# Moving the kv sums next to other small matmuls, and z into 128x64 tiles, in a fused sketched-attention and GELU kernel

## The chip, the cores and the metric

The kernel runs on one core of a Trainium2 chip. The metric is the device time of one execution, in microseconds (us). Engines are called by the names of the profile: PE is TensorE, DVE is VectorE, ACT is ScalarE, POOL is GpSimd, SP is SyncE. PE multiplies matrices into PSUM, and a second row of the profile, PEld, shows its weight loads.

A float32 matmul of the kernel appears in the profile as two records. "128*64" in a row gives the tile of PE's array that a matmul uses: 128 rows (the length of the sum) by 64 columns (rows of the output). Two matmuls in 128*64 tiles, four in 128*32 tiles or eight in 64*32 tiles lie side by side in the array.

## The reference

Attention with polynomial sketches, and then a dense layer with GELU:

```python
def phi(x):                                   # x: (4, 4, 1088, 32), r = 8
    a = np.einsum('rd,bhsd->bhsr', S1, x)
    b = np.einsum('rd,bhsd->bhsr', S2, x)
    return np.einsum('bhsi,bhsj->bhsij', a, b).reshape(*x.shape[:-1], r * r)
q_p, k_p = phi(q), phi(k)
kv = np.einsum('bhsf,bhsd->bhfd', k_p, v)     # 64 x 32 for each batch and head
z = np.sum(k_p, axis=2)                       # 64 for each batch and head
num = np.einsum('bhsf,bhfd->bhsd', q_p, kv)
den = np.einsum('bhsf,bhf->bhs', q_p, z)[..., None] + 1e-06
x = num / den                                 # then (4352, 128)
h = x @ w_in                                  # (4352, 2048)
out = (0.5 * h * (1 + erf(h / sqrt(2)))) @ w_out
```

There are 4 batches (B) and 4 heads (H) of width 32 (D); F = 64 is the number of features, and a batch has 1088 tokens.

## The kernel before

**Chunks and steps.** Tokens are taken in nine chunks n. Chunks 0 to 7 have 512 tokens, two of them for each batch; chunk 8 holds the 64 remaining tokens of all batches. For each chunk the hidden layer is made in 16 slices fi of 128 channels. A step t is one slice of one chunk: `hidden` (line 686) multiplies a slice of w_in by the chunk's transposed activations xT into a PSUM bank h_ps (line 692, from step 18 on in two 128*64 halves), and ACT applies GELU to it (line 699). Chunks 0 and 1 share the first 32 steps; chunk n from 2 on has the steps 16n to 16n + 15. There are two h_ps banks, so the hidden of step t needs the gelu of step t - 2.

**The second layer.** From four gelu slices (a block) POOL makes four sums (`token_sums`, lines 741 to 744), and PE multiplies blocks and sums by parts of w_out in pairs of 128*64 matmuls (`two_products`, line 776). These products come some steps later, at the end of a step. DVE adds them up and stores the chunk.

**Attention.** For batches 1 to 3, `features_of_all` (line 945, 64*32 tiles) sketches a batch's keys, and DVE makes their features k_p (`outer_of_all`, lines 953 to 960) and their sum over the tokens of one partition, k_s (`add_tokens`, lines 969 to 975). PE then forms, head by head,

- kv: `kv_sum` (line 431), 32 + 4 matmuls in 128*32 tiles, 72 records, all through `kv_product` (line 428);
- z, spread over a head's 32 rows: `z_sum` (line 440), a matmul of 128*32 for each head, with ones as its stationary part and k_s as its moving part.

ACT copies kv out of PSUM (`take_kv`, line 453), PE turns it with an identity (`turn_kv`, line 458, 128*64) and ACT copies the result to kz (line 459). DVE multiplies z into the sketch weights (`fold_z`, which calls `sketch_of_z`, lines 483 to 486), and the result, S_abc, is the stationary part of `query_sketch` (line 568, 64*32 tiles). So a chunk's sketch also gives its denominators. `query_outer` (from line 580 on, DVE) makes the features of the queries, already divided; `attend` (line 617, 64*32 tiles) multiplies them by kz, and ACT copies the numerators to xT (line 623). Batch 0 has another way at the start; its z is turned by `turn_first_kv` (line 504) for use in chunk 8.

**Order.** Every engine keeps the order of the program text. A table of slots, filled by `at(t, ...)`, says what is issued in step t besides hidden and the products: in a step come the hidden matmul, then the slots in the order in which they were entered, then the products. Batch 1 has its entries in steps 12 to 28: `features_of_all`, `outer_of_all` in 16, `add_tokens` in 17, kv in 21, `turn_kv` in 22, z and `fold_z` in 23, `query_sketch` of chunk 2 in 24. For batches 2 and 3 the entries are relative to t = 32 and 64: kv and z at t + 13 in one function, `turn_kv` and `fold_z` at t + 14. An even chunk n has `attend` of chunk n - 1 and `query_sketch` of chunk n in the step before its first one; an odd one has `sketch_and_attend` there.

**PSUM.** There are eight banks: two h_ps, two o_ps for the products, and two pairs w_ps for all else (`work_banks`; `work_bank` gives the first of a pair). A third user of w_ps waits until one of the pairs is done with.

Of the kernel before, what the change touches and what calls it, by code (L numbers as in the profile page):

```python
# [8 lines left out]
FP = mybir.dt.float32  # L9
# [7 lines left out]
def kernel(  # L17
# [18 lines left out]
    pe, dve, act, pool, sp = nc.tensor, nc.vector, nc.scalar, nc.gpsimd, nc.sync  # L36
    B, H, S, D = q.shape
    R = S1.shape[0]
    F = R * R
# [3 lines left out]
    NP = H // 2  # L43
# [4 lines left out]
    CW = JC * 128  # L48
    G = 128 // 32
    NCH = J // JC  # L50
# [9 lines left out]
    big = ctx.enter_context(tc.tile_pool(name="big", bufs=1))  # L60
# [6 lines left out]
    def work_banks():  # L67

        return wps.tile([128, 2, CW], FP, name="w_ps")

    def work_bank():
        return work_banks()[:, 0]
# [7 lines left out]
    def out_bank():  # L80
        return ops.tile([128, CW], FP, name="o_ps")
# [137 lines left out]
    ident = big.tile([128, 128], FP, name="ident")  # L219
# [9 lines left out]

    kz_first = big.tile([128, 128], FP, name="kz_first")  # L230

    ones = big.tile([128, D], FP, name="ones")

    v_rem_aug = [big.tile([128, H, D if b else 2 * D], FP, name=f"v_rem_aug{b}") for b in range(B)]
    pool.memset(v_rem_aug[0], 0.0)
    pool.memset(v_rem_aug[0][:REM], 1.0)
    dve.memset(ones, 1.0)

    v_aug = [att.tile([128, NP, J, 2 * D], FP, name="sums") for r in range(2)]
    for t in v_aug:  # L240
# [165 lines left out]
    k_s = {}  # L406

    def flat(features):
        return features.rearrange("p i j -> p (i j)")
# [16 lines left out]
    def kv_product(ps, lhsT, features, h, part, start=False, stop=False):  # L426

        pe.matmul(ps[h * D:(h + 1) * D, part * F:(part + 1) * F], lhsT=lhsT, rhs=features, start=start, stop=stop,  # L428
                  skip_group_check=True)

    def kv_sum(b, ps):


        for i in range(J):
            for h in range(H):
                kv_product(ps, main["v", b][:, h, i, :], k_p[b][h // 2][:, i, h % 2], h, 0, start=i == 0)
        for h in range(H):
            kv_product(ps, v_rem_aug[b][:, h, :], flat(k_p_rem[b % 2][:, h]), h, 0, stop=True)

    def z_sum(b):  # L440

        ps = held["kv"][:, 0]
        for h in range(H):
            kv_product(ps, ones, k_s[b][:, h], h, 1, start=True, stop=True)

    def fold_z(b):
        sketch_of_z(b, held["kv"][:, 0], F)

    kv_T = {}

    def take_kv(b, ps):
        kv_T[b] = att.tile([128, F], FP, name="kv_T")
        act.copy(out=kv_T[b], in_=ps[:, :F])

    def turn_kv(b, banks):

        for rows in (slice(0, 64), slice(64, 128)):
            pe.matmul(banks[rows, 1, :128], lhsT=kv_T[b], rhs=ident, start=True, stop=True)
        act.copy(out=kz[b], in_=banks[:, 1, :128])
# [20 lines left out]
    def sketch_of_z(b, ps, at):  # L480

        zs = att.tile([128, R, R], FP, name="z_s")
        dve.tensor_mul(out=zs, in0=ps[:, at:at + F].rearrange("p (i j) -> p i j", i=R), in1=sT[:, None, R:].broadcast_to([128, R, R]))
        c = ps[:, 2 * F:2 * F + R]
        dve.tensor_reduce(out=c, in_=zs, axis=mybir.AxisListType.X, op=AX.add)
        dve.tensor_mul(out=S_abc[b][:, :, :, 4:8], in0=c.rearrange("p (i f) -> p i f", i=2)[:, :, None].broadcast_to([128, 2, 2, 4]),
                       in1=own_r[:, None, :, None].broadcast_to([128, 2, 2, 4]))
# [11 lines left out]
    def turn_first_kv():  # L499

        ps, zs = work_bank(), held["zs"]
        for h in range(H):
            c, r = h // 2, h % 2
            pe.matmul(ps[h * D:(h + 1) * D, :F], lhsT=zs[:, r], rhs=ident[:, c * F:(c + 1) * F], start=True, stop=True)
        sketch_of_z(0, ps, 0)


# [44 lines left out]
    def batch_of(n, s, i):  # L552
        return n // NCH if n < NMAIN else i * 2 + s
# [51 lines left out]
    def attend(n, banks=None):  # L605


        W = width[n]
        m = 1 if n < NMAIN else B // 2
        banks = work_banks() if banks is None else banks  # L610
        f = qp[n].rearrange("f r x -> f (r x)")[:, :2 * W].rearrange("f (c i n r t) -> f c i n r t", c=NP, i=m, r=2, t=32)
        N = W // 2 // m
        for i in range(m):
            for s in range(2):
                rows, b = slice(s * 64, (s + 1) * 64), batch_of(n, s, i)
                for h in range(H):
                    pe.matmul(banks[h * D:(h + 1) * D, s, i * N:(i + 1) * N],  # L617
                              lhsT=(kz[b] if b else kz_first)[rows, h * D:(h + 1) * D],
                              rhs=f[rows, h // 2, i, :, h % 2], start=True, stop=True)
        xT[n] = att.tile([128, CW], FP, name="xT", bufs=3)  # L620
        to = xT[n][:, :W]
        to = to.rearrange("p (s x) -> p s x", s=2) if m == 1 else to.rearrange("p (s t i) -> p s i t", s=2, i=m)
        act.copy(out=to, in_=banks[:, :, :W // 2] if m == 1 else banks[:, :, :W // 2].rearrange("p s (i t) -> p s i t", i=m))
# [238 lines left out]
    r = Rounding(SR)  # L862
# [12 lines left out]
    banks = [out_bank(), out_bank()]  # L875
# [59 lines left out]
    def at(t, f, *a):  # L935
        slots[t].append(lambda: f(*a))
# [40 lines left out]
    held = {}  # L977
# [11 lines left out]
    def features_rem(pair):  # L989
        key_features_rem(pair, held["rem"])  # L990

    def finish_keys(b, z=True):
        held["kv"] = work_banks()
        kv_sum(b, held["kv"][:, 0])
        if z:
            z_sum(b)
        take_kv(b, held["kv"][:, 0])

    def round_at(t, w, product_by=dve):
        r = []  # L1000
# [18 lines left out]
    at(17, add_tokens, 1)  # L1019
    at(18, channel_sums, 4)  # L1020

    at(21, finish_keys, 1, False)
    at(22, lambda: turn_kv(1, held["kv"]))
    at(23, z_sum, 1)
    at(23, fold_z, 1)
    at(23, query_turn, 3)
    at(24, query_sketch, 2)
    at(24, query_outer, 2)
    for i, t in enumerate((25, 26, 28)):
        at(t, channel_sums, i)  # L1030
# [2 lines left out]
    for n in range(3, NCHUNK):  # L1033

        t = (n - 1) * NF
        b = (n + 1) // 2
        keys = n % 2 and b < B
        if n > 3:
            at(t - 6, query_turn, n)
        if keys:  # L1040
            at(t - 1, sketch_and_attend, n)
            at(t - 1, features_of_all, b)
        else:
            at(t - 1, attend, n - 1)
            at(t - 1, query_sketch, n)
        at(t - 1, query_outer, n)
        if keys:
            for r in range(2):
                at(t - 3 if n > 3 else t - 4, key_turn_blocks, b, r)

        if n == NMAIN:
            at(t + 15, attend, n)
        if keys:
            at(t + 5 + (n == NCH + 1), outer_of_all, b)
            at(t + 5 + (n == NCH + 1), add_tokens, b)
            at(t + 8, widen_v_rem, b)
            at(t + 13, finish_keys, b)
            if b == 2:
                at(t + 13, turn_first_kv)
            at(t + 14, lambda b=b: turn_kv(b, held["kv"]))  # L1060
            at(t + 14, fold_z, b)


    products = {t: [] for t in range(len(steps) + LAG)}
# [2 lines left out]
    for t, (n, fi) in enumerate(steps):  # L1067
# [13 lines left out]
        elif fi % NB == NB - 1:  # L1081
            b = fi // NB
# [11 lines left out]
    for t in range(len(steps) + LAG):  # L1094
        if t < 4:
# [9 lines left out]
            if t == 3:  # L1105
                banks = work_banks()
# [23 lines left out]
        if t < len(steps):  # L1130
            n, fi = steps[t]
            hidden(n, fi, by_halves=t >= 18 and (n < NMAIN or fi < 5))
        if t < len(steps) and steps[t][0] < NMAIN and steps[t][1] % NB == NB - 1:
            n, b = steps[t][0], steps[t][1] // NB
# [50 lines left out]
```

## Time and profile before

| | |
|---|---|
| time, median of 3 runs | 260.33 us (260.18 to 260.61) |
| time of the profiled execution | 260.86 us |
| its span, first to last instruction | 259.1 us |
| granted clock of PE, mean | 0.999 |
| PE busy | 254.6 us, 98% of the span |
| POOL busy | 163.5 us, 63% |
| DVE busy | 151.6 us, 59% |
| ACT busy | 114.9 us, 44% |
| L428, kv and its remainder: 192 + 24 records of 128*32, 64 columns | 3.3 + 0.9 us |
| L428, z: 24 records of 128*32, 64 columns | 0.9 us |
| L504, turn of the first z: 8 records of 128*32, 64 columns | 0.3 us |
| L568, sketches of queries: 96 records of 64*32, 256 columns | 3.9 us |
| L617, numerators: 96 records of 64*32, 256 columns | 3.9 us |

The span is what the instructions cover; the execution's time has some 1.8 us more around it. Matmuls overlap: the ends in the profile are modelled, and what a group of matmuls takes from PE is read from the starts. A timeline gives start and length in us, engine, line, operation, the tiles written and read, the shape, the number of instructions merged into the row, and in brackets idle time of the engine and what ended it.

### The profile page before, as it was taken

The numbers are of one execution on the slowest core, as the hardware profiler recorded it, in microseconds if no ns is written. First come the engines' busy times: TensorE is split into PE (matmuls) and PEld (weight loads), VectorE is DVE, ScalarE is ACT, GpSimd is POOL, SyncE is SP. The second block draws the span as 40 slices with busy tenths as digits, with TensorE's granted clock in tenths as the row PEclk, the third lists the DMA queues.
The fourth block names the chain that finished last, engine by engine and source line by source line (L and its number), as shares of the span: only waits on it lengthen the run. The fifth ranks groups of instructions, "written<-read, shape, count | busy, mean of one in ns | idle before, by whom it ended". The sixth has DMA issues, their size and how long they took to land.

```text
span 259.1 us, 5758 instructions
## 1 busy us (share of the span) xinstructions
PE 254.6 (98%) x2335; PEld 134.8 (52%) x2335; DVE 151.6 (59%) x313; ACT 114.9 (44%) x221; POOL 163.5 (63%) x173
## 2 busy tenths in 40 slices
PE   8999999999999999999999999999999999999994
PEld 7856444344444554444444454444445444445794
DVE  2886879969698997680178957630565043600330
ACT  4675767432625333533335334533353335334431
POOL 3404006799968776687758766867768776877200
PEclk9999999999999999999999999999999999999999
DMA  6469849820000101001000011020001100010020
GB/s 205 137 192 360 206 95 220 217 54 13 3 0 13 30 4 28 13 12 31 3 0 3 0 27 17 3 41 0 3 0 25 19 4 0 14 29 0 3 41 20
DMA packets 29530, 13.48 MB, mean 52 GB/s; under 512 B 21824, under 2 KB 27712, under 8 KB 29504
## 3 DMA queue, kind: packets, MB, share of 16 engines
q1 hardware_dynamic: 29472, 13.12, 20.8%
q8 instruction: 18, 0.29, 0.5%
q14 instruction: 8, 0.07, 0.1%
q10 hardware_dynamic: 32, 0.00, 0.0%
HBM read 10.88 MB, written 2.23 MB: 51 GB/s over the span
## 4 chain that ended last, share of the span: by engine, by line
PE 98%; ACT 0%; issue 0%; DVE 0%
PE h_ps L692 45%; PE o_ps L776 33%; PE o_ps L827 5%; PE w_ps L824 3%; PE w_ps L428 2%; PE w_ps L857 1%; PE w_ps L617 1%; PE w_ps L568 1%; PE o_ps L417 1%; PE w_ps L534 1%; PE h_ps L706 1%; PE h_ps L333 1%; PE w_ps L945 1%; PE w_ps L635 0%; PE w_ps L333 0%; PE h_ps L373 0%
## 5 line engine op out<-in xcount | busy, mean ns | idle before, releaser
L692 PE MATMUL h_ps<-xT,w_in 128*64 128x512 f32 (+3 forms) x514 | 137.1, 576 | 0.0
L699 ACT ACTIVATE block<-h_ps 128x512 f32<-128x512 f32 (+1 forms) x128 | 73.0, 571 | 120.2 <-PE h_ps L692 119.8
L776 PE MATMUL o_ps<-block,w_out 128*64 128x256 f32 x224 | 57.5, 379 | 0.0
L692 PEld LDWEIGHTS h_ps<-xT,w_in 128*64 128x64 f32 (+1 forms) x514 | 41.9, 142 | 29.2 <-issue 11.6
L741 POOL TENSOR_TENSOR bits_low<-block 128x512 f32<-128x512 f32 x28 | 35.6, 1273 | 27.6 <-ACT block L699 27.6
L776 PEld LDWEIGHTS o_ps<-block,w_out 128*64 128x64 f32 x224 | 30.5, 137 | 37.5 <-issue 26.7
L742 POOL TENSOR_TENSOR bits_a<-block 128x512 f32<-128x512 f32 x28 | 35.7, 1276 | 12.8 <-ACT block L699 12.8
L743 POOL TENSOR_TENSOR bits_e<-bits_a,block 128x512 f32<-128x512 f32 x28 | 36.1, 1290 | 2.2
L744 POOL TENSOR_TENSOR bits_m<-block,bits_e 128x512 f32<-128x512 f32 x28 | 35.8, 1280 | 2.2
L580 DVE STREAM_TRANSPOSE w_ps<-w_ps 128x512 f32<-128x512 f32 (+1 forms) x7 | 4.9, 693 | 42.8 <-PE w_ps L568 30.1
L776 PE MATMUL o_ps<-bits_low,small 128*64 128x256 f32 x112 | 29.0, 381 | 0.0
L776 PE MATMUL o_ps<-block,small 128*64 128x256 f32 x112 | 28.9, 381 | 0.0
L776 PE MATMUL o_ps<-bits_a,small 128*64 128x256 f32 x112 | 28.8, 379 | 0.0
L776 PE MATMUL o_ps<-bits_m,w_out 128*64 128x256 f32 x112 | 28.7, 379 | 0.0
L776 PEld LDWEIGHTS o_ps<-block,small 128*64 128x64 f32 x112 | 15.0, 137 | 17.6 <-issue 10.2
L791 DVE COPY sums<-o_ps 64x256 f32<-64x256 f32 x8 | 3.3, 416 | 34.4 <-PE o_ps L776 34.4
L776 PE MATMUL o_ps<-bits_e,small 128*64 128x256 f32 x112 | 17.1, 384 | 0.0
L827 PE MATMUL o_ps<-g,w_out 128*128 128x512 f32 (+1 forms) x34 | 16.5, 572 | 0.0
L776 PEld LDWEIGHTS o_ps<-bits_m,w_out 128*64 128x64 f32 x112 | 15.3, 137 | 0.0
L776 PEld LDWEIGHTS o_ps<-bits_a,small 128*64 128x64 f32 x112 | 15.2, 137 | 0.0
L776 PEld LDWEIGHTS o_ps<-bits_low,small 128*64 128x64 f32 x112 | 15.0, 137 | 0.0
L776 PEld LDWEIGHTS o_ps<-bits_e,small 128*64 128x64 f32 x112 | 7.5, 136 | 10.6 <-issue 9.1
(181 smaller groups left out, 303.2 us busy)
## 6 DMA issues: line engine op xcount, KB each, us to landing
out_dram<-oT SPq DMA_DIRECT2D x26, 64.0 KB, 2.2
block<-in_moe_w_in_dram SPq DMA_DIRECT2D x3, 512.0 KB, 7.2
block<-in_moe_w_out_dram SPq DMA_DIRECT2D x3, 512.0 KB, 11.6
k<-in_k_dram SPq DMA_DIRECT2D x12, 128.0 KB, 2.8
v<-in_v_dram SPq DMA_DIRECT2D x12, 128.0 KB, 3.4
q<-in_q_dram SPq DMA_DIRECT2D x24, 64.0 KB, 2.3
k<-in_k_dram SPq DMA_DIRECT2D x2, 256.0 KB, 2.8
q<-in_q_dram SPq DMA_DIRECT2D x2, 256.0 KB, 4.1
```

Source lines behind the costliest of these rows:

```text
L428: pe.matmul(ps[h * D:(h + 1) * D, part * F:(part + 1) * F], lhsT=lhsT, rhs=features, start=start, stop=stop, skip_group_check=True)
L580: dve.transpose(out=tok, in_=ps[:, :, :H2])
L692: pe.matmul(ps[rows, :W], lhsT=w[:, rows], rhs=xT[n][:, :W], start=True, stop=True)
L699: act.activation(out=g_of[n, fi][:, :W], in_=ps[:, :W], func=ACT.Gelu)
L741: pool.tensor_sub(out=s[3], in0=a11, in1=a21)
L742: pool.tensor_add(out=s[1], in0=a21, in1=a22)
L743: pool.tensor_sub(out=s[2], in0=s[1], in1=a11)
L744: pool.tensor_sub(out=s[4], in0=a12, in1=s[2])
L776: pe.matmul(acc[n][bank][half * 64:(half + 1) * 64, col:col + HW], lhsT=fixed, rhs=moving, start=opens and e == 0 and name in "4715", stop ...
L791: dve.tensor_copy(out=N[lo, 0, one], in_=a0[lo, one])
L824: pe.matmul(o_of[n][i][:, :128], lhsT=g[:, i * 128:(i + 1) * 128], rhs=w_tile(w_out_sb, fi), start=first, stop=final)
L827: pe.matmul(o_of[n][:, cols], lhsT=w_tile(w_out_sb, fi), rhs=g[:, cols], start=first, stop=final)
```

## The change

kv and z of a batch are no longer one function. kv is issued directly ahead of other matmuls in 32-column tiles, into a free part of their PSUM pair: in step 24 ahead of `query_sketch` of chunk 2 (batch 1), and in the steps 47 and 79 ahead of `attend` of chunks 3 and 5, which `query_sketch` of chunks 4 and 6 follows (batches 2 and 3). `turn_kv` comes two steps after it, instead of one.

z stays in step 23 for batch 1 and in steps 45 and 77 for the others, with a PSUM pair of its own. Its stationary part is now 64 columns wide: ones for one head of a pair and noughts for the other, and the two matmuls of a pair are added up in PSUM, so that there are still four matmuls. `fold_z` follows in the same step. The turn of the first z goes from four matmuls with 32 columns to two with 64, one step later.

```diff
--- before.py
+++ after.py
@@ -229,12 +229,13 @@
 
     kz_first = big.tile([128, 128], FP, name="kz_first")
 
-    ones = big.tile([128, D], FP, name="ones")
+    ones = big.tile([128, 3, D], FP, name="ones")
 
     v_rem_aug = [big.tile([128, H, D if b else 2 * D], FP, name=f"v_rem_aug{b}") for b in range(B)]
     pool.memset(v_rem_aug[0], 0.0)
     pool.memset(v_rem_aug[0][:REM], 1.0)
-    dve.memset(ones, 1.0)
+    dve.memset(ones, 0.0)
+    dve.memset(ones[:, 1], 1.0)
 
     v_aug = [att.tile([128, NP, J, 2 * D], FP, name="sums") for r in range(2)]
     for t in v_aug:
@@ -439,12 +440,14 @@
 
     def z_sum(b):
 
-        ps = held["kv"][:, 0]
-        for h in range(H):
-            kv_product(ps, ones, k_s[b][:, h], h, 1, start=True, stop=True)
+        held["z"] = work_bank()
+        for r in range(2):
+            for c in range(NP):
+                pe.matmul(held["z"][c * F:(c + 1) * F, :F], lhsT=ones[:, 1 - r:3 - r].rearrange("p a d -> p (a d)"),
+                          rhs=k_s[b][:, 2 * c + r], start=r == 0, stop=r == 1)
 
     def fold_z(b):
-        sketch_of_z(b, held["kv"][:, 0], F)
+        sketch_of_z(b, held["z"], 0)
 
     kv_T = {}
 
@@ -499,9 +502,9 @@
     def turn_first_kv():
 
         ps, zs = work_bank(), held["zs"]
-        for h in range(H):
-            c, r = h // 2, h % 2
-            pe.matmul(ps[h * D:(h + 1) * D, :F], lhsT=zs[:, r], rhs=ident[:, c * F:(c + 1) * F], start=True, stop=True)
+        for c in range(NP):
+            pe.matmul(ps[c * F:(c + 1) * F, :F], lhsT=zs.rearrange("f r d -> f (r d)"), rhs=ident[:, c * F:(c + 1) * F],
+                      start=True, stop=True)
         sketch_of_z(0, ps, 0)
 
 
@@ -989,12 +992,13 @@
     def features_rem(pair):
         key_features_rem(pair, held["rem"])
 
-    def finish_keys(b, z=True):
-        held["kv"] = work_banks()
-        kv_sum(b, held["kv"][:, 0])
-        if z:
-            z_sum(b)
-        take_kv(b, held["kv"][:, 0])
+    def kv_and_attend(b, n):
+
+        banks = held["kv"] = work_banks()
+        kv_sum(b, banks[:, 1, CW // 2:])
+        if n >= NCH:
+            attend(n, banks)
+        take_kv(b, banks[:, 1, CW // 2:])
 
     def round_at(t, w, product_by=dve):
         r = []
@@ -1019,12 +1023,12 @@
     at(17, add_tokens, 1)
     at(18, channel_sums, 4)
 
-    at(21, finish_keys, 1, False)
-    at(22, lambda: turn_kv(1, held["kv"]))
     at(23, z_sum, 1)
     at(23, fold_z, 1)
     at(23, query_turn, 3)
+    at(24, kv_and_attend, 1, 1)
     at(24, query_sketch, 2)
+    at(26, lambda: turn_kv(1, held["kv"]))
     at(24, query_outer, 2)
     for i, t in enumerate((25, 26, 28)):
         at(t, channel_sums, i)
@@ -1033,7 +1037,7 @@
     for n in range(3, NCHUNK):
 
         t = (n - 1) * NF
-        b = (n + 1) // 2
+        b = (n + 1) // 2 if n % 2 else n // 2
         keys = n % 2 and b < B
         if n > 3:
             at(t - 6, query_turn, n)
@@ -1041,7 +1045,11 @@
             at(t - 1, sketch_and_attend, n)
             at(t - 1, features_of_all, b)
         else:
-            at(t - 1, attend, n - 1)
+            if n % 2 == 0 and b < B:
+                at(t - 1, kv_and_attend, b, n - 1)
+                at(t + 1, lambda b=b: turn_kv(b, held["kv"]))
+            else:
+                at(t - 1, attend, n - 1)
             at(t - 1, query_sketch, n)
         at(t - 1, query_outer, n)
         if keys:
@@ -1054,11 +1062,10 @@
             at(t + 5 + (n == NCH + 1), outer_of_all, b)
             at(t + 5 + (n == NCH + 1), add_tokens, b)
             at(t + 8, widen_v_rem, b)
-            at(t + 13, finish_keys, b)
+            at(t + 13, z_sum, b)
+            at(t + 13, fold_z, b)
             if b == 2:
-                at(t + 13, turn_first_kv)
-            at(t + 14, lambda b=b: turn_kv(b, held["kv"]))
-            at(t + 14, fold_z, b)
+                at(t + 14, turn_first_kv)
 
 
     products = {t: [] for t in range(len(steps) + LAG)}
```

## The prediction

> **What bounds the kernel now.** I read the page first: TensorE carries the chain that ended last, so a change counts by what it adds to or takes from PE's own queue, or by letting PE stand still.
>
> ```profile
> PE 254.6 (98%) x2335; PEld 134.8 (52%) x2335; DVE 151.6 (59%) x313; ACT 114.9 (44%) x221; POOL 163.5 (63%) x173
> ...
> PE 98%; ACT 0%; issue 0%; DVE 0%
> ```
>
> Second, PE's timeline where batch 1 is finished (steps 21 to 25). Columns: start, length, then what ran; the time that a run of matmuls holds PE is the distance to the next start, since ends overlap.
>
> ```profile
> 50.28 1.06 PE L692 MATMUL h_ps<-xT,w_in 128*64 128x512 f32 x4
> 51.27 1.10 PE L428 MATMUL w_ps<-k_p,v 128*32 128x64 f32 x64
> 52.19 0.29 PE L428 MATMUL w_ps<-k_p_rem,v_rem_aug 128*32 128x64 f32 x8
> 52.41 1.08 PE L692 MATMUL h_ps<-xT,w_in 128*64 128x512 f32 x4
> 53.32 0.39 PE L458 MATMUL w_ps<-ident,kv_T 128*64 128x128 f32 x4
> 53.54 1.03 PE L692 MATMUL h_ps<-xT,w_in 128*64 128x512 f32 x4
> 54.50 0.32 PE L428 MATMUL w_ps<-k_s,ones 128*32 128x64 f32 x8
> 54.75 0.43 PE L776 MATMUL o_ps<-block,small 128*64 128x256 f32 x1
> ...
> 56.09 1.03 PE L692 MATMUL h_ps<-xT,w_in 128*64 128x512 f32 x4
> 57.05 0.66 PE L568 MATMUL w_ps<-qT,S_abc 64*32 64x256 f32 x16
> 57.65 0.43 PE L776 MATMUL o_ps<-block,w_out 128*64 128x256 f32 x1
> ```
>
> To be seen: no gap anywhere, and the price of a tile size. Four hidden records (L692) take 0.86 among 128*64 work (58.56 to 59.42); 0.96 ahead of another size (53.54 to 54.50); 0.91 just after one (52.41 to 53.32). The kv run is 18 groups of four records; 64 of them take 0.92, which is 0.056 a group and 0.02 at the start, so 1.01 of work, and the run holds PE 1.14.
>
> Third, VectorE's timeline in the same place, which decides this forecast.
>
> ```profile
> 49.07 4.07 DVE L969 TENSOR_REDUCE w_ps<-k_p 128x128 f32<-128x1024 f32 x2
> 53.18 0.43 DVE L974 COPY k_s<-w_ps 64x256 f32<-64x256 f32 x1
> 53.62 0.42 DVE L975 TENSOR_TENSOR k_s<-w_ps,k_p_rem 64x256 f32<-64x256 f32 x1
> 54.96 0.22 DVE L483 TENSOR_TENSOR z_s<-w_ps,sT 128x64 f32<-128x64 f32 x1 [0.92 <-PE w_ps L428]
> ```
>
> The token sums k_s of batch 1, which z multiplies, are ready at 53.62 + 0.42 = 54.04. VectorE has had no idle time since the transpose at 44.67, all of it fed by PE work before 47. z starts on PE at 54.50, some 0.4 after its operand.
>
> **What the Trainium skill says.** "TensorEngine Tiling (Array Packing)", Tiling Modes, Key Properties: changing the tiling mode drains TensorE. The trace agrees: 0.10 before, 0.13 to 0.16 at the other end, 0.05 in the first pair after it. "TensorE: Matmul & The Clock Gate", Part 1 (engine queue depths): PE may pull weight loads ahead, but matmuls stay in order. So nothing behind a waiting z can pass it; that a wait stops the queue isn't seen here, since PE hardly waits. Same page and part: the clock falls only after about 3.4 us without work. The granted clock is 9 tenths or more in all slices; the wait that I expect is a third of that.
>
> **The change, part by part.**
>
> *Price of a separate small run.* 128*32 (kv, z): 0.10 before + 0.02 in its first group + 0.11 at its end + 0.05 after = 0.29. 64*32 (sketches): L568 holds PE 0.60 for 0.43 of work (69.01 to 69.44 is a run in the middle of such work), so 0.10 + 0.16 + 0.05 = 0.31.
>
> *kv beside sketches or numerators (three times).* The 72 records stay. Two separate runs cost 0.29 + 0.31 = 0.60. Merged, there are three switches: into 128*32 (0.12), from 128*32 to 64*32 (unknown), out (0.14 + 0.05). The unknown is not in the trace. Below: 0, if only the rows are split and the columns stay 32. Above: 0.14, the 0.11 at the end of a kv run and 0.025 for the next start. Nearest row: from 64*64 to 32*64, also a change of rows alone:
>
> ```profile
> 12.11 0.67 PE L635 MATMUL h_ps<-kz,q_pT 64*64 64x33 f32 x32
> 12.60 0.65 PE L635 MATMUL o_ps<-kz,q_pT 64*64 64x33 f32 x32
> 13.17 0.69 PE L534 MATMUL w_ps<-qT,Srep 32*64 32x256 f32 x16
> ```
>
> The first 32 records take 0.49, with a switch at their start; the last 32 take 0.57 with one at their end. A change of rows alone is therefore not free (about 0.11). I take 0.14: each merge saves 0.60 − 0.45 = 0.15.
>
> *z in 128x64 tiles.* Still 8 records, now in two tiles instead of four: four pairs instead of two groups. L417 (128*64, 33 columns) runs 16 pairs from 10.16 to 11.16, 0.06 a pair, so z is 0.24. For batch 1 it loses a run of its own: 0.11 + 0.29 = 0.40 before, 0.24 after, −0.16. For batches 2 and 3, where z stood inside the kv run: +0.13 each. The turn of the first z goes from 8 records to 4: two pairs for two groups, 0.12 for 0.11, nothing.
>
> *The cover that z loses.* kv (1.14 + 0.10 + 0.05) leaves step 21 and turn_kv (53.32 to 53.54, 0.22) leaves step 22; both stood ahead of z(1) in PE's queue, which stays in step 23. Hidden of step 21 ends at 51.27 − 0.10 = 51.17; two more at 0.86 bring PE to z at 52.9, or 53.1 if step 23 must wait for the bank of step 21's gelu (it ends about 52.1). But k_s is there only at 54.04, since VectorE's work is the same. With 0.1 to wake, z starts at 54.15: **PE stands about 1.1 us**, and with it the products of step 23, the hidden of 24, kv and the sketches. ACT's next gelu waits for these; POOL's token sums (gapless from 49.34 to 59) have their inputs.
>
> *Batch 1 summed.* z from 54.15, 0.03 for an unloaded start, 0.24: products start at 54.42, not 54.75 (−0.33). They no longer follow a switch (−0.05). kv comes ahead of the sketches (+1.14, their 0.60 unchanged): the sketches end 0.76 later. turn_kv in step 26: +0.22. **+0.98**.
>
> *Batches 2 and 3.* k_s is ready at 93.05 and 148.47, z came at 95.29 and 151.5 and would come at 94.3 and 150.4: no wait. Each −0.15 + 0.13: **−0.02**, twice.
>
> *Costed at nothing.* The second memset of ones (0.09 like the first): VectorE then waits 2.54 for S; without that, 0.1. The copy kv_T on ACT (0.21) follows the copy xT that hidden needs, and turn_kv comes two steps later; if it came before, up to 0.2. query_outer(2) ends 0.76 later, at 65.0, and its features are used at about 70. fold_z: only a query transpose (0.71) is queued behind it. Banks: in batch 2 the first z's fold ended at 99.08 and kv needs a bank at 99.4; it should get that of z, free at 98.6. No DMA moves, SP and POOL get nothing new.
>
> Sum: 0.98 − 0.04 = +0.94. The profiled execution (260.86, span 259.1) becomes 261.8 with a span of 260.0; on the median 260.33, which is 0.53 below the profiled one, **261.25**.
>
> **The rivals.**
> A, as above: 261.25, own range 260.95 to 261.6.
> B, z waits but the rows-only switch is free: 3 × 0.14 less, +0.52, 260.85. Same columns speak for it, the rows above against.
> C, z(1) doesn't wait: then only the switches count, 0.98 becomes −0.31, in all −0.36: 259.97, not slower. Its place is k_s against the end of hidden in step 23. The point: the sum is nought when the wait is 0.2 instead of 1.1, that is with k_s by about 53.2. VectorE's unbroken chain speaks against it, as does z's slack of only 0.4.
> D, one more wait: kv or the sketches of batches 2 and 3 find their bank not yet freed by the folds, which VectorE ends 0.2 to 0.8 before (99.08 against 99.4): up to 0.5 in all, 261.7. Against: both engines shift together.
>
> **How the numbers follow.** A 0.66, B 0.12, C 0.10, D 0.12. About 0.2% (0.5 us) is what a measurement of this kernel tells from no change. Slower: A, D and a part of B, 0.80; same: the rest of B and most of C, 0.16; faster 0.04 (C with a free switch, 259.55). Range 260.7 to 261.7: A, most of B and half of D, with 0.1 to 0.2 either way for the median.
>
> **What would show it.** The timeline after: L692 of steps 18 to 23 with no L428 between; a gap of 1.0 to 1.2 before L428 with k_s, put down to VectorE's k_s (L975) and not to an issue; L428 of kv followed by L568 after about 1.14, or 1.01 if B is right; L504 with 4 records; batches 2 and 3 without gaps. I am wrong if k_s is ready earlier, if PE is busy until 54, or if the gap lies elsewhere.

## The result and the profile after

The changed kernel takes 262.4 us (median of 6 runs, 261.68 to 262.63), the kernel before on the same chip 260.56 (6 runs, 260.18 to 261.15). The ratio is 1.0067 with a 95% interval from 1.0050 to 1.0084: slower by about 1.75 us by that ratio, which is not simply the quotient of the two medians. The forecast was 261.25, with a range of 260.7 to 261.7. The direction was right, the forecast size was about half of the measured one, and the measured time lies above the range. The profiled execution took 262.53 us and has a span of 260.7.

The page of the changed kernel, busy times and the chain that ended last:

```profile
PE 254.8 (98%) x2331; PEld 135.4 (52%) x2331; DVE 151.6 (58%) x314; ACT 114.8 (44%) x221; POOL 163.3 (63%) x173
...
PE 92%; DVE 5%; issue 1%; ACT 1%; DVEq 0%
```

PE is as busy as before, in absolute terms. What changed is the chain: it was 98% PE, now 5% of it runs over VectorE. So PE has begun to wait for VectorE. Busy shares alone would not have shown it.

Lines have moved: in the kernel after z is L446, kv L429, hidden L695, the products L779, the sketches L571, the numerators L620, `turn_kv` L461, the second half of k_s L978 and the end of a fold L489.

PE's timeline where batch 1 is finished, kernel after (start, length, what ran, idle time before and what ended it):

```profile
50.42 2.94 PE L695 MATMUL h_ps<-xT,w_in 128*64 128x512 f32 x12
54.17 0.45 PE L446 MATMUL w_ps<-k_s,ones 128*64 128x64 f32 x8 [0.81 <-DVE k_s L978]
54.45 0.38 PE L779 MATMUL o_ps<-block,small 128*64 128x256 f32 x1
...
55.75 1.03 PE L695 MATMUL h_ps<-xT,w_in 128*64 128x512 f32 x4
56.71 1.10 PE L429 MATMUL w_ps<-k_p,v 128*32 128x64 f32 x64
...
57.85 0.45 PE L571 MATMUL w_ps<-qT,S_abc 64*32 64x256 f32 x8
```

The same from 53.2 on, where the first row holds the last two hidden matmuls alone, and VectorE's timeline beside it:

```profile
52.76 0.60 PE L695 MATMUL h_ps<-xT,w_in 128*64 128x512 f32 x2
```

```profile
53.70 0.42 DVE L978 TENSOR_TENSOR k_s<-w_ps,k_p_rem 64x256 f32<-64x256 f32 x1
```

This is the forecast wait: the hidden matmuls run through without kv between them. The last two of them start at 52.76 and take 0.43 (half of the 0.86 for four), so z could follow at 53.19. It starts at 54.17, 0.05 after the end of k_s (53.70 + 0.42). PE stands 0.98. The bracket says 0.81, since the lengths of matmuls are modelled and reach beyond the next possible start. kv follows further down, and from its start to that of the sketches it takes 57.85 − 56.71 = 1.14, what it took ahead of 128*64 work before. So the change from 128*32 to 64*32, rows alone, costs here what a change of columns cost.

The second wait is in batch 2. The kernel before first, PE's timeline and one row of VectorE's, the end of the fold of batch 2's z:

```profile
94.26 1.10 PE L428 MATMUL w_ps<-k_p,v 128*32 128x64 f32 x64
...
95.63 0.43 PE L776 MATMUL o_ps<-block,small 128*64 128x256 f32 x1
...
97.40 0.39 PE L458 MATMUL w_ps<-ident,kv_T 128*64 128x128 f32 x4
...
99.44 0.66 PE L617 MATMUL w_ps<-q_pT,kz 64*32 64x256 f32 x16
```

```profile
98.47 0.17 DVE L486 TENSOR_TENSOR S_abc<-w_ps,own_r 128x16 f32<-128x16 f32 x1
```

The same of the kernel after:

```profile
98.11 1.03 PE L695 MATMUL h_ps<-xT,w_in 128*64 128x512 f32 x4
99.75 1.10 PE L429 MATMUL w_ps<-k_p,v 128*32 128x64 f32 x64 [0.60 <-PE h_ps L695]
...
100.89 0.66 PE L620 MATMUL w_ps<-q_pT,kz 64*32 64x256 f32 x16
```

Its VectorE, and its row of PE's sequencer at line 429 between 94 and 101 (durations in ns: shortest, median, longest):

```profile
98.13 0.71 DVE L841 STREAM_TRANSPOSE oT<-sums 128x512 f32<-128x512 f32 x1
98.88 0.23 DVE L486 TENSOR_TENSOR z_s<-w_ps,sT 128x64 f32<-128x64 f32 x1
99.14 0.23 DVE L488 TENSOR_REDUCE w_ps<-z_s 128x8 f32<-128x64 f32 x1
99.47 0.17 DVE L489 TENSOR_TENSOR S_abc<-w_ps,own_r 128x16 f32<-128x16 f32 x1
99.56 0.21 DVE L486 TENSOR_TENSOR z_s<-w_ps,sT 128x64 f32<-128x64 f32 x1
```

```profile
L429 PEldq EVENT_SEMAPHORE  x3: 51/51/3177, 96.3 to 96.5; - x3
```

Four hidden records ahead of another tile size take 0.96, here 1.63 (98.11 to 99.75): PE stands 0.67. The sequencer held a semaphore for 3.18 us, from 96.5 to 99.69. Just before that, at 99.64 (99.47 + 0.17), VectorE ended the fold of batch 2's z (the first L489); the fold of the first z, which begins at 99.56, was still running when kv started. The bracket names PE's own hidden work as the releaser, which isn't it: hidden was done by 99.14 (98.11 + 1.03). The wait was for several semaphores, and by its time that of VectorE came last; an experiment below tests it. z had taken one pair of w_ps, the first z the other, and kv had to wait until VectorE had read z's. VectorE came to it late, since it stored chunk 1 first (up to L841).

Where the 1.64 us between the two spans are, from the starts of PE's work at the same points in both: 0.14 up to step 18 (the start, of which the experiments say more), 0.88 in batch 1, 0.65 in batch 2, −0.03 in batch 3. Between these points the two kernels keep step.

### The profile page after: what moved, and what is told of

Same layout as the page of the kernel before. It is cut to its first block, busy times and chain, and to the rows that moved or that the text cites. A ratio compares the mean times of both kernels' runs of the same rounds, so it can differ in the third digit from the quotient of the medians.

```text
span 260.7 us, 5752 instructions
## 1 busy us (share of the span) xinstructions
PE 254.8 (98%) x2331; PEld 135.4 (52%) x2331; DVE 151.6 (58%) x314; ACT 114.8 (44%) x221; POOL 163.3 (63%) x173
## 4 chain that ended last, share of the span: by engine, by line
PE 92%; DVE 5%; issue 1%; ACT 1%; DVEq 0%
PE h_ps L695 41%; PE o_ps L779 33%; PE o_ps L830 4%; PE w_ps L827 3%; DVE w_ps L972 2%; PE w_ps L860 1%; PE w_ps L620 1%; PE w_ps L571 1%; PE w_ps L429 1%; DVE k_p L963 1%; PE o_ps L418 1%; PE w_ps L537 1%; PE h_ps L709 1%; PE h_ps L334 1%; DVE kT L360 0%
## 5 line engine op out<-in xcount | busy, mean ns | idle before, releaser
L695 PE MATMUL h_ps<-xT,w_in 128*64 128x512 f32 (+3 forms) x514 | 136.9, 576 | 0.0
L695 PEld LDWEIGHTS h_ps<-xT,w_in 128*64 128x64 f32 (+1 forms) x514 | 41.8, 142 | 30.6 <-issue 11.6
L779 PE MATMUL o_ps<-block,w_out 128*64 128x256 f32 x224 | 57.5, 379 | 0.0
L779 PEld LDWEIGHTS o_ps<-block,w_out 128*64 128x64 f32 x224 | 30.5, 137 | 38.0 <-issue 27.5
L779 PE MATMUL o_ps<-bits_low,small 128*64 128x256 f32 x112 | 28.8, 380 | 0.0
L779 PE MATMUL o_ps<-block,small 128*64 128x256 f32 x112 | 28.8, 380 | 0.0
L779 PE MATMUL o_ps<-bits_a,small 128*64 128x256 f32 x112 | 28.8, 379 | 0.0
L779 PE MATMUL o_ps<-bits_m,w_out 128*64 128x256 f32 x112 | 28.7, 379 | 0.0
L779 PEld LDWEIGHTS o_ps<-block,small 128*64 128x64 f32 x112 | 14.9, 137 | 15.6 <-issue 8.5
L779 PE MATMUL o_ps<-bits_e,small 128*64 128x256 f32 x112 | 17.1, 384 | 0.0
L779 PEld LDWEIGHTS o_ps<-bits_m,w_out 128*64 128x64 f32 x112 | 15.3, 137 | 0.0
L779 PEld LDWEIGHTS o_ps<-bits_a,small 128*64 128x64 f32 x112 | 15.2, 137 | 0.0
L779 PEld LDWEIGHTS o_ps<-bits_low,small 128*64 128x64 f32 x112 | 14.9, 137 | 0.0
L779 PEld LDWEIGHTS o_ps<-bits_e,small 128*64 128x64 f32 x112 | 7.5, 136 | 10.5 <-issue 8.7
```

The lines of the kernel that those rows point to most:

```text
L695: pe.matmul(ps[rows, :W], lhsT=w[:, rows], rhs=xT[n][:, :W], start=True, stop=True)
L779: pe.matmul(acc[n][bank][half * 64:(half + 1) * 64, col:col + HW], lhsT=fixed, rhs=moving, start=opens and e == 0 and name in "4715", stop ...
```

## The experiments

Theory: PE loses 0.98 at z of batch 1, where kv and its turn had been the cover for k_s (PE's own work, during which VectorE finished k_s), and 0.67 at kv of batch 2, where a pair of w_ps comes free late. Rivals: the smaller runs and the 64-column z are dear in themselves; or PE waits at these places for something else.

Beside the measured ratio to the kernel before on the same chip, with its 95% interval, I give the length of PE's queue: from its first 128*64 hidden (step 18, 47.53 in the kernel before) to the first product after the sketches of chunk 8 (210.50). All places of the change lie in it, the start-up doesn't. It is 162.96 us before and 164.46 after, so +1.50; when two profiles were taken of one kernel they agree within 0.01.

**The changed kernel again**, without an edit, on the chip of the three that follow.

> The changed kernel itself, so that the others are compared on the same chip. Both theories: 1.5 to 2.0 us over the kernel before. In the profile: PE stands about 1.0 us ahead of z of batch 1 and about 0.7 us ahead of kv of batch 2, and nowhere else by more than 0.1.

Ratio 1.0065 (1.0051 to 1.0078), 262.27 against 260.84 us. Queue +1.50, with both waits as before. The start-up's 0.14 didn't come back: step 18 began at 47.48 here, 0.05 ahead of the kernel before's. In the ten profiles of this study it lies between 46.87 and 48.06, and it differs for one kernel profiled twice (47.62 and 47.80 with both moves), so I take none of it for an effect of the change.

**z of batch 1 a step later.**

```diff
-    at(23, z_sum, 1)
-    at(23, fold_z, 1)
     at(23, query_turn, 3)
+    at(24, z_sum, 1)
+    at(24, fold_z, 1)
     at(24, kv_and_attend, 1, 1)
```

> z and fold_z of batch 1 go from step 23 to step 24, ahead of kv; k_s is then long there. Theory of two waits (PE waits 0.98 for k_s at z of batch 1 and 0.67 at kv of batch 2): the first wait goes and nothing else, so 0.9 to 1.0 us less than the changed kernel, 0.5 to 0.9 over the kernel before. Rival (the loss lies in the small tiles' own cost, merged runs and 64-column z): all of that is still there, so it stays 1.5 to 2.0 over. Rival (the wait only moves, to the sketches that need fold_z): a gap of about 1 us ahead of the sketches instead.

Ratio 1.0030 (1.0018 to 1.0042), 261.43 us; queue +0.47, 1.03 less than the changed kernel. PE's timeline at z:

```profile
54.10 1.03 PE L695 MATMUL h_ps<-xT,w_in 128*64 128x512 f32 x4
54.96 0.40 PE L446 MATMUL w_ps<-k_s,ones 128*64 128x64 f32 x8
```

z follows hidden after 0.86. The first wait is gone, 0.98 of the 1.03 (the rest, 0.05, is what z took longer after the wait: 0.28 instead of 0.23). There is no new wait at the sketches, which follow kv after the same 1.14. Batch 2 still waits 0.67.

**The turn of the first z after kv of batch 2.**

```diff
-                at(t + 14, turn_first_kv)
+                at(t + 18, turn_first_kv)
```

> The turn of the first z goes from step 46 to step 50, so that z of batch 2 has one w_ps pair, kv the other, and kv needs no pair that VectorE has still to read. Theory (kv of batch 2 waits for the pair of z, which VectorE frees only after storing chunk 1): 0.6 to 0.7 us less than the changed kernel, 0.8 to 1.3 over the kernel before, and kv follows the hidden of step 47 without a gap. Rival (kv waits for another of VectorE's or POOL's results, such as features or the widened v): the gap of 0.67 stays.

Ratio 1.0032 (1.0021 to 1.0044), 261.54 us; queue +0.82, 0.68 less than the changed kernel. PE's timeline, and then the end of z's fold on VectorE:

```profile
97.20 1.03 PE L695 MATMUL h_ps<-xT,w_in 128*64 128x512 f32 x4
98.16 1.10 PE L429 MATMUL w_ps<-k_p,v 128*32 128x64 f32 x64
```

```profile
98.67 0.17 DVE L489 TENSOR_TENSOR S_abc<-w_ps,own_r 128x16 f32<-128x16 f32 x1
```

kv follows hidden after the usual 0.96, and it starts 0.68 before VectorE is done with z. So it was the pair: not the features, not v, and not that fold itself, none of which the edit makes earlier. In batch 1 the wait for k_s remained: from step 18 to the product after the sketches of chunk 2 it takes 10.77, as in the changed kernel.

**Both moves.**

> Both moves together. Theory of two waits: they add up, 1.6 us less than the changed kernel, within 0.3 of the kernel before, on either side. The three merges and the 64-column z then stand alone, worth 0.1 to 0.4. Rival (small tiles' own cost): 1 us or more over the kernel before.

Ratio 0.9988 (0.9981 to 0.9995), 260.43 us; queue −0.21. The two gains add up: 1.03 + 0.68 = 1.71, and 1.50 − 1.71 = −0.21. The same kernel on the chip of the next runs:

> The kernel with both moves once more, beside z_in_run on the same chip: within 0.3 us of the kernel before; 0.1 to 0.3 over z_in_run if z's place in the run is worth what the records say.

Ratio 0.9992 (0.9984 to 1.0000), 260.62 us; queue −0.21. So without the two waits the change gains 0.2 us. The merges and the wide z alone gain more: 0.17 is lost again in the steps 22 and 23, which wait for ACT's gelus when no kv lies between them. This excludes the rival that the small tiles' own cost makes the loss.

**kv of batch 1 back in its step.**

```diff
-    at(24, kv_and_attend, 1, 1)
+    at(21, kv_and_attend, 1, 1)
     at(24, query_sketch, 2)
-    at(26, lambda: turn_kv(1, held["kv"]))
+    at(22, lambda: turn_kv(1, held["kv"]))
```

> kv of batch 1 goes back to step 21 and its turn to step 22; z keeps its step and its 64 columns, and all of batches 2 and 3 stays as changed. Theory of the lost cover: with 1.3 us of work back ahead of it z finds k_s ready; the wait goes, batch 1 is about 0.15 faster than in the kernel before, and the wait of batch 2 (0.67) stays: 0.4 to 0.8 over the kernel before. Rival (z in 128x64 tiles is itself slow): 1.5 over.

Ratio 1.0026 (1.0015 to 1.0037), 261.55 us; queue +0.45. PE's timeline:

```profile
53.53 1.03 PE L695 MATMUL h_ps<-xT,w_in 128*64 128x512 f32 x4
54.39 0.40 PE L446 MATMUL w_ps<-k_s,ones 128*64 128x64 f32 x8
54.62 0.38 PE L779 MATMUL o_ps<-block,small 128*64 128x256 f32 x1
```

With its cover back z follows hidden after 0.86 and takes 0.23, with no gap and no change of size: up to the products of chunk 2's sketches PE is 0.17 ahead of the kernel before, where z was a run of its own. k_s was ready at the same time as in the kernel before (53.62 + 0.42), and the 0.67 of batch 2 stays.

**k_s sooner, with PE's order untouched.**

```diff
-    at(15, query_turn, 2)
...
     at(17, add_tokens, 1)
+    at(18, query_turn, 2)
```

> VectorE's transpose of the queries of chunk 2 (0.65 us in its queue) goes from ahead of batch 1's features to behind its token sums, so k_s is ready 0.65 us sooner; PE's order is untouched. Theory of the lost cover: the wait at z of batch 1 shrinks by as much, from 0.98 to about 0.33, and the time by 0.65: 0.9 to 1.2 over the kernel before. Rival (the wait is for something else than k_s, such as a PSUM pair or ACT): no change, 1.5 to 2.0 over.

Ratio 1.0036 (1.0023 to 1.0049), 261.56 us; queue +0.90, 0.60 less than the changed kernel. PE's timeline at z:

```profile
53.68 0.45 PE L446 MATMUL w_ps<-k_s,ones 128*64 128x64 f32 x8 [0.20 <-DVE k_s L978]
```

Counted from step 18, k_s was 0.61 sooner and the wait was 0.60 shorter (a bracket of 0.20 instead of 0.81). So the wait follows k_s one to one.

**z in its old form at the head of the merged run.** The edit takes up z of all three batches, with the first z's turn in step 50.

```diff
     def kv_and_attend(b, n):
+        z_sum(b)
+        fold_z(b)
         banks = held["kv"] = work_banks()
...
     def z_sum(b):
         held["z"] = work_bank()
-        for r in range(2):
-            for c in range(NP):
-                pe.matmul(held["z"][c * F:(c + 1) * F, :F], lhsT=ones[:, 1 - r:3 - r].rearrange("p a d -> p (a d)"),
-                          rhs=k_s[b][:, 2 * c + r], start=r == 0, stop=r == 1)
+        for h in range(H):
+            kv_product(held["z"], ones[:, 1], k_s[b][:, h], h, 0, start=True, stop=True)
...
-            at(t + 13, z_sum, b)
-            at(t + 13, fold_z, b)
```

and the two entries of batch 1 in step 23 go.

> z in its old form, four matmuls of 128x32, directly ahead of kv in the merged run of each batch, and fold_z with it; the first z's turn in step 50. No z of its own among the 128*64 work: 0.11 instead of 0.23 us for each batch, three times. Theory: no wait for k_s; a wait of 0.1 to 0.2 in batch 1, where only kv covers fold_z ahead of the sketches, none in batches 2 and 3, where the numerators lie between. 0.1 to 0.3 less than with both moves, 0.2 to 0.6 less than the kernel before. Rival (fold_z's 0.9 us isn't covered): each batch waits 0.5 or more at its sketches, and it is slower than the kernel before.

Ratio 0.9974 (0.9967 to 0.9981), 260.18 us against 260.78; queue −0.52, 0.31 less than with both moves. By the queue this is the fastest of all, and it beats the kernel before by 0.6 us in the medians. Its batch 2, PE and then VectorE (its lines behind z's are two lower than in the changed kernel, and z goes through L429 again):

```profile
98.01 0.32 PE L429 MATMUL w_ps<-k_s,ones 128*32 128x64 f32 x8
98.14 1.08 PE L429 MATMUL w_ps<-k_p,v 128*32 128x64 f32 x64
...
99.26 0.66 PE L618 MATMUL w_ps<-q_pT,kz 64*32 64x256 f32 x16
99.72 0.64 PE L569 MATMUL w_ps<-qT,S_abc 64*32 64x256 f32 x16
```

```profile
98.99 0.17 DVE L487 TENSOR_TENSOR S_abc<-w_ps,own_r 128x16 f32<-128x16 f32 x1
```

z adds 0.11 to the run and none of its own to the products. Its fold ends at 99.16, 0.56 before the sketches that use it, under the cover of kv and the numerators. In batch 1, with kv alone as cover, the run was 0.04 longer than in batch 2, less than the expected wait of 0.1 to 0.2.

## Why the prediction was right in its direction and half of its size

**Right: the wait of z in batch 1.** The place, the cause, the operand and its line were as forecast. Nothing passed the waiting z: the products start at 54.45, behind it, though with z moved away they started right behind hidden (with both moves at 53.14, which is 53.19 on this clock). The Trainium skill says so in "TensorE: Matmul & The Clock Gate", Part 2, Step-by-step: matmuls stay in program order, and only weight loads are pulled ahead. (The prediction named Part 1 for both; that part has the weight loads alone.) The clock stayed granted in full (mean 1.0). The stretch was forecast at +0.98 and was +0.88. The wait was 0.98 and not 1.1: k_s came 0.06 sooner counted from step 18, and z started 0.05 after it, not 0.1. PE reached z at 53.05 on the clock of the kernel before, between the 52.9 and 53.1 of the prediction, since steps 22 and 23, without kv between them, are held up by ACT's gelus (that of step 21 ended at 52.23, and the hidden of step 23 starts at 52.28). The six hidden steps 18 to 23 take 5.52 instead of 5.15 (six at 0.858); those of the kernel before lose 0.20 in steps 18 to 21, so another 0.17 is lost in 22 and 23. The prediction had set 0 to 0.2 for this. In its rival C, without a wait, it left this term out: batch 1 was to come to −0.31 there, and with both moves it came to −0.15.

**Right: the prices of tile sizes.** The switch of rows alone was taken at its upper bound, 0.14, and took that (1.14 from kv to the sketches, as from kv to 128*64 work before); that it was just the bound is in part luck, for the nearest row had given about 0.11. With it fell rival B. What the Trainium skill says in "TensorEngine Tiling (Array Packing)", Tiling Modes, Key Properties, that a change of mode drains TensorE, agrees with this price for rows alone. z in two tiles took 0.23 for a forecast 0.24 where it didn't wait, the first z 0.11 for 0.12. Batch 3 came to −0.03 for −0.02, batch 1 without its wait to −0.17 with kv in place, for −0.16. Rival C was excluded by the profile itself. Two sums of the prediction are off by 0.01 (0.28, not 0.29, for a separate 128*32 run, and −0.35, not −0.36, for C), which changes nothing.

**Wrong: batch 2, forecast at −0.02, measured +0.65.** The step that failed is the sentence under "Costed at nothing" that kv needs a bank at 99.4 and gets one free at 98.6, and the same margin in rival D. (The 99.08 that it compares with 99.4 is the start of the last instruction of the first z's fold, which ended at 99.25; what counted was the pair of batch 2's z, free at 98.64.) The 99.4 is where the numerators stood in the kernel before, *behind* a run of kv and z in step 45 and a turn in step 46. The change takes just these away from ahead of them. Worked as batch 1 was worked: 99.44 less 1.37 for the run (94.26 to 95.63), 0.15 for its entry and the pair after it, 0.22 for the turn, plus the forecast 0.24 and 0.12 for the two z's, gives 98.06. VectorE frees the pair at 98.64; with 0.05 to 0.1 to wake, a wait of 0.6 to 0.7. It was 0.67. All these numbers could be had from the trace of before. So rival D, held at 0.12 and at most 0.5, came true on top of A, in batch 2 alone. The argument against it, that both engines shift together, is true for what comes from batch 1 (hidden of step 45 started 1.01 later than before, and the fold of z ended 1.00 later), but leaves out that PE alone is moved by what is taken out in batch 2.

So the lost cover acts at two places, and I had applied it at one. The remaining −0.02 of batch 2 is right: 0.65 − 0.67. In all, 0.98 − 0.02 − 0.02 = 0.94 was forecast, and PE's queue shows 0.88 + 0.65 − 0.03 = 1.50.

The queue's +1.50 is less than the 1.75 of the ratio. The rest, about 0.25, lies ahead of step 18 or within the interval (1.3 to 2.2 us); as the start-up varies by more than that from profile to profile, I don't assign it.

## What to carry to other kernels

A small run that costs PE time can be the cover for another engine's result; when it is moved, every operand and every buffer that the work behind it needs must be dated anew, from the kernel after and not from the starts of the kernel before. A pool with two buffers makes the order of allocations a part of the schedule: a user of little urgency, taken just before an urgent one, gives it the buffer that is freed last, and a move of four steps removed the wait. And where a result is used soon but needs little time of another engine, as z's fold does here, its maker did best at the head of the run that covers it, in that run's tile size, and not in a run of its own.

## What the runs showed of the hardware

A change of PE's tile size cost the same with rows alone as with columns: from 128*32 to 64*32 the kv run held PE 1.14 us, as it did from 128*32 to 128*64. And the stretch of PE's queue from step 18 on, waits included, repeats to a few ns: 162.755 us in both profiles of the kernel with both moves, and 164.459 and 164.464 in the two of the changed kernel. The 47 us ahead of it differed by up to 1.2 us between the ten profiles, and by 0.2 between two of one kernel. For changes of a few tenths this stretch tells more than the ratios, whose intervals reach 0.2 to 0.4 us to either side.
